# Sketched attention and a squared-ReLU MLP on one core: denominators from a Gram matrix, x made transposed in 32x32 array tiles, and one written order for all engines

## The chip, the core and the metric

The kernel runs on one core of a Trainium2 chip. The core has five engines with instruction queues of their own: PE (matrix multiply; it writes to PSUM), DVE and ACT (both read PSUM and SBUF), POOL (does not read PSUM here) and SP (issues DMAs). ACT and POOL issue DMAs too. Engines wait for one another by semaphores, and each runs its own instructions in order. The metric is the device time of one execution in microseconds; the number for a kernel is the median over runs.

## The reference, cut to what matters

```python
batch, n_heads, seq, head_dim, r = 4, 4, 1088, 32, 8      # q, k, v: float32

def phi(x):
    a = einsum('rd,bhsd->bhsr', S1, x)
    b = einsum('rd,bhsd->bhsr', S2, x)
    return einsum('bhsi,bhsj->bhsij', a, b).reshape(..., r * r)

q_p, k_p = phi(q), phi(k)
kv  = einsum('bhsf,bhsd->bhfd', k_p, v)
z   = sum(k_p, axis=2)
num = einsum('bhsf,bhfd->bhsd', q_p, kv)
den = einsum('bhsf,bhf->bhs', q_p, z)[..., None] + 1e-06
x   = (num / den) transposed to [4352, 128]                # 4 heads x 32
out = square(maximum(x @ w_in, 0)) @ w_out                 # d_ff 2048
```

Since `z` summed over the keys is the 8x8 matrix G of products of `a` and `b` of the keys, `den` is also a(q)ᵀ G b(q).

## The kernel before

Of 1088 = 34 x 32 tokens of a batch, 32 x 32 go in two chunks of 512 and the last 2 x 32 of every batch are collected in a ninth chunk of 256 (`ci` 0 to 8).

**Keys** (`k_stage`, once per batch). DVE transposes k in 32x32 blocks (L149, L154). PE projects it on S1 and S2 (L175, f32, outputs on 64 partitions). ACT copies the `a` half out of PSUM (L190) and DVE multiplies it with the `b` half into 64 features (L191). v is copied beside a column of ones (`v_pad`, L198 and L200, POOL after batch 0), and PE sums features times [v, 1] over the keys with the features stationary (L209, 128 rows by 32 columns of the array, 33 moving columns): the 33rd column is z. POOL (ACT and DVE in batch 0) spreads the sums into `KV` (L229).

**Queries** (`q_feat`). DVE transposes q (L149, L154), PE projects with the stationary Wq and 512 moving columns (L260), DVE transposes the result out of PSUM (L266), forms the 64 features (L268) and transposes them (L276) into `qp`.

**Output of attention** (`q_out`). PE multiplies qp and KV in 64x64 tiles (L298, 66 moving columns: two heads of 32 values and a denominator). DVE adds 1e-6, takes reciprocals and scales (L312 to L315) into bf16, PE transposes (L324), ACT copies to `xT` (L330).

**MLP** (`f_stage`, nine chunks, eight units of two 128-wide blocks of d_ff). PE makes h (L355, bf16, 512 moving columns), ACT applies Relu from PSUM to bf16 (L362), DVE squares four blocks at a time (L366, 2048 columns), PE accumulates the output (L371, 16 matmuls per square), ACT copies it out (L381), and four DMAs on SP store it (L384; the last chunk's are L389). `h_ps` has two buffers of two PSUM banks, `r_sb` and `g_sb` three each, `o_ps` one.

**Order.** A generator runs attention steps between MLP units (80 steps spread over the units); the framework's scheduler orders each engine, with chains for the matmuls of a step. Loads go on SP batch by batch: k, six pieces of v, q. POOL issues the weights (L111, L112), which are converted to bf16 on the way, after a one-element copy from v of batch 0 (L110); another from the weights into k of batch 1 (L113) holds the later loads on SP until the weights are in.

Of the kernel before, what the change touches and what calls it, by code (L numbers as in the profile page):

```python
# [19 lines left out]

@with_exitstack
def kernel(
# [11 lines left out]
    nc = tc.nc  # L34
    NOSYNC = mybir.DependencyInfo(mybir.DependencyClass.NoSync, mybir.DependencyReason.DATA)

    def chain(insts):

        for x, y in zip(insts, insts[1:]):
            tc.add_manual_dep(y.ins, x.ins.name, NOSYNC, reason="chain")  # L40

# [3 lines left out]
    F = r * r  # L45
# [4 lines left out]
    VW = D + 1  # L50
    assert (B, H, D, r, NJ) == (4, 4, 32, 8, 34)

    consts = ctx.enter_context(tc.tile_pool(name="consts", bufs=1))
    kin = ctx.enter_context(tc.tile_pool(name="kin", bufs=1))
    kTp = ctx.enter_context(tc.tile_pool(name="kTp", bufs=2))
    vin = ctx.enter_context(tc.tile_pool(name="vin", bufs=1))
    kab_pool = ctx.enter_context(tc.tile_pool(name="kab", bufs=2))
    kp_pool = ctx.enter_context(tc.tile_pool(name="kp", bufs=2))
    a_pool = ctx.enter_context(tc.tile_pool(name="arep", bufs=3))
    qp_pool = ctx.enter_context(tc.tile_pool(name="qp", bufs=3))  # L60
    den_pool = ctx.enter_context(tc.tile_pool(name="den", bufs=3))
    xb_pool = ctx.enter_context(tc.tile_pool(name="xb", bufs=2))
    xT_pool = ctx.enter_context(tc.tile_pool(name="xT", bufs=4))
    r_pool = ctx.enter_context(tc.tile_pool(name="r", bufs=3))
    g_pool = ctx.enter_context(tc.tile_pool(name="g", bufs=3))
    osb_pool = ctx.enter_context(tc.tile_pool(name="osb", bufs=2))
    ps_h = ctx.enter_context(tc.tile_pool(name="ps_h", bufs=2, space=PSUM))
    ps_o = ctx.enter_context(tc.tile_pool(name="ps_o", bufs=1, space=PSUM))
    ps_m = ctx.enter_context(tc.tile_pool(name="ps_m", bufs=3, space=PSUM))

    warm = consts.tile([128, 1], F32)
    nc.vector.memset(warm, 0.0)
    nc.scalar.activation(warm, warm, ACTF.Relu)
# [5 lines left out]
    nc.scalar.dma_start(out=S12[:r, 0, :], in_=S1)  # L79
    nc.scalar.dma_start(out=S12[r:, 0, :], in_=S2)  # L80

    kin_t, qin_t, vraw, vpad = {}, {}, {}, {}
    for b in range(B):
        kin_t[b] = kin.tile([128, NJ, D], F32, tag=f"k{b}", name="k_in")
        qin_t[b] = kin.tile([128, NJ, D], F32, tag=f"q{b}", name="q_in")
        vraw[b] = vin.tile([128, H, NLO + 1, D], F32, tag=f"v{b}", name="v_in")
        vpad[b] = vin.tile([128, H, NLO + 1, VW], F32, tag=f"vp{b}", name="v_pad")
    w_in_sb = consts.tile([128, C_TILES, 128], BF16)
    w_out_sb = consts.tile([128, C_TILES, 128], BF16)

    def load(b):
        nc.sync.dma_start(out=kin_t[b], in_=k[b].rearrange("h (t j) d -> (h t) j d", j=NJ))
        for h in range(H):
            vr = v[b, h].rearrange("(t j) d -> t j d", j=NJ)[:, : 4 * NLO, :]
            nc.sync.dma_start(  # L95
                out=vraw[b][:, h, :NLO, :],
                in_=vr.rearrange("t (i l) d -> i t (l d)", i=4),
            )
        for j2 in range(2):
            nc.sync.dma_start(  # L100
                out=vraw[b][32 * j2 : 32 * (j2 + 1), :, NLO, :],
                in_=v[b].rearrange("h (t j) d -> j t h d", j=NJ)[32 + j2],
            )
        nc.sync.dma_start(out=qin_t[b], in_=q[b].rearrange("h (t j) d -> (h t) j d", j=NJ))

    load(0)

    for b in range(B):
        nc.gpsimd.memset(vpad[b][:, :, :, D:VW], 1.0)
    nc.gpsimd.tensor_copy(w_in_sb[:1, 0, :1], vraw[0][:1, H - 1, 0, :1])  # L110
    nc.gpsimd.dma_start(out=w_in_sb, in_=moe_w_in.rearrange("d (ct c) -> d ct c", c=128))  # L111
    nc.gpsimd.dma_start(out=w_out_sb, in_=moe_w_out.rearrange("(ct c) d -> c ct d", c=128))  # L112
    nc.gpsimd.tensor_copy(kin_t[1][:1, 0, :1], w_in_sb[:1, 0, :1])  # L113
    for b in range(1, B):
        load(b)


    ident_b = consts.tile([128, 128], BF16)
    nc.vector.tensor_copy(ident_b, ident)
    mask = consts.tile([128, H], F32)  # L120
    nc.vector.memset(mask, 0.0)
    for h in range(H):
        nc.vector.memset(mask[32 * h : 32 * (h + 1), h : h + 1], 1.0)
    nc.vector.tensor_copy(
        S12[:, 1:, :], S12[:, 0:1, :].to_broadcast([2 * r, H - 1, D])
# [6 lines left out]
    nc.vector.tensor_tensor(  # L132
        out=Wk,
        in0=T_ps[:, None, : 2 * r].to_broadcast([128, H, 2 * r]),
        in1=mask[:, :, None].to_broadcast([128, H, 2 * r]),
        op=ALU.mult,
    )
    Wq = consts.tile([128, H, 32], F32)
    nc.vector.memset(Wq, 0.0)
    nc.vector.tensor_copy(Wq[:, :, : 2 * r], Wk)  # L140
    KV = consts.tile([128, B, 2, 2, VW], F32)
    nc.vector.memset(KV, 0.0)
    KV0 = 360
    qT_rem = consts.tile([128, B, 64], F32)
    qT_all = {}

    def block_transpose(dst, dst_rem, src):
        pin(
            nc.vector.transpose(  # L149
                dst.rearrange("p (l h t) -> p l h t", l=NLO, h=4),  # L150
# [3 lines left out]
        pin(nc.vector.transpose(dst_rem, src[:, 4 * NLO :, :]))  # L154


    def k_stage(b):

        kt = kTp.tile([128, S], F32, tag="kT", name="kT")
        block_transpose(  # L160
            kt[:, :1024], kt[:, 1024:].rearrange("p (j t) -> p j t", j=2), kin_t.pop(b)
        )
        vt = vpad[b]
        eng = nc.scalar.copy if b == 0 else nc.gpsimd.tensor_copy
        yield
        tiles = ([(m, 128) for m in range(4)], [(m, 128) for m in range(4)] + [(4, 64)])
        kks, kps, seqs = {}, {}, ([], [])

        def project(gi):
            kks[gi] = kk = ps_m.tile([128, 512], F32, tag="m", name="kab_ps")  # L170
            for m, P in tiles[gi]:
                c0 = (4 * gi + m) * 128
                for c in range(P // 64):
                    seqs[gi].append(
                        nc.tensor.matmul(  # L175
                            kk[64 * c : 64 * c + 64, m * 64 : (m + 1) * 64],
                            kt[:, c0 + 64 * c : c0 + 64 * c + 64],
                            Wk.rearrange("p h x -> p (h x)"),
                            start=True,
                            stop=True,  # L180
                        )
                    )

        def features(gi):
            kk = kks[gi]
            ka = kab_pool.tile([128, 5 * H, r], F32, tag="ka", name="ka")
            kps[gi] = kp = kp_pool.tile([128, 5 * H, r, r], F32, tag="kp", name="kp")
            for P, g0, g1 in ((128, 0, 4 * H), (64, 4 * H, 5 * H))[: gi + 1]:
                kabv = kk[:P, g0 * 2 * r : g1 * 2 * r].rearrange("p (g x) -> p g x", x=2 * r)
                nc.scalar.copy(ka[:P, g0:g1], kabv[:, :, :r])  # L190
                nc.vector.tensor_tensor(  # L191
                    out=kp[:P, g0:g1],
                    in0=ka[:P, g0:g1, :, None].to_broadcast([P, g1 - g0, r, r]),
                    in1=kabv[:, :, None, r:].to_broadcast([P, g1 - g0, r, r]),
                    op=ALU.mult,
                )
            n0 = 4 * gi
            pin(eng(vt[:, :, n0 : n0 + 4, :D], vraw[b][:, :, n0 : n0 + 4, :]))  # L198
            if gi:
                pin(eng(vt[:64, :, NLO, :D], vraw[b][:64, :, NLO, :]))  # L200

        def sums(gi):
            kp, seq = kps[gi], seqs[gi]
            kv = kks[0][:, KV0 : KV0 + 2 * VW].rearrange("p (f w) -> p f w", f=2)
            for m, P in tiles[gi]:
                for f in range(2):
                    for h in range(H):
                        seq.append(
                            nc.tensor.matmul(  # L209
                                kv[32 * h : 32 * h + 32, f],  # L210
                                kp[:P, m * H + h, 4 * f : 4 * f + 4].rearrange(
                                    "p i j -> p (i j)"
                                ),
                                vt[:P, h, 4 * gi + m, :],
                                start=(gi == 0 and m == 0 and f == 0),
                                stop=(gi == 1 and m == len(tiles[1]) - 1 and f == 1),
                            )
                        )
            if gi:
                if b:  # L220
# [243 lines left out]
```

## Time and profile before

| what | value |
| --- | --- |
| median of 3 runs | 145.01 us (144.13 to 145.67) |
| profiled execution | 145.95 us, of which the span is 143.8 us |
| granted TensorE clock | 0.997 |
| moved by DMA | 8.78 MB read, 2.23 MB written |

The span runs from the first instruction to the end of the last store; the execution's own time is 2.15 us longer. "Busy" is the union of an engine's instructions, so overlapped ones count once. In a group's row the two numbers before the second bar are the busy time of the group and the mean of one instruction in ns, and after it stands the idle time just before the group and what ended it. An f32 matmul appears as two records.

| group | count | mean ns of one |
| --- | --- | --- |
| h, L355, 512 columns bf16 | 112 records | 390 |
| output, L371, 128 columns bf16 | 544 | 219 |
| nd, L298, 64x64 tiles, 66 columns f32 | 544 | 234 |
| key sums, L209, 128x32 tiles, 33 columns f32 | 512 | 210 |
| Relu, L362, 1024 columns | 64 | 1031 |
| square, L366, 2048 columns | 32 | 1221 |
| key features, L191, 1024 columns f32 | 8 | 1210 |
| query features, L268, 1024 columns f32 | 8 | 1296 |
| query feature transposes, L276, 1024 columns f32 | 8 | 1238 |

Matmuls overlap, so their rate is read from rows of the timeline, in which consecutive instructions of a kind are merged, and not from these means.

### The profile page before, as it was taken

Reading aid. Unit: us, or ns where it says so; the run is one execution under the profiler, and the core shown is the slowest. Engines: PE = TensorE matmul, PEld = TensorE weight load, DVE = VectorE, ACT = ScalarE, POOL = GpSimd, SP = SyncE. Lnnn points to the kernel's source line nnn. Section 1 sums busy time; section 2 is a strip of 40 time slices with the busy share of each in tenths; the row PEclk is TensorE's granted clock in tenths of the full one; section 3 lists DMA queues with packets and bytes.
Section 4 is the critical chain, followed back from the end, with each engine's and each line's share of the span. In section 5 each row is a group of like instructions: output and inputs, shape, how many; then the busy total and the mean of one; then the engine's idle time right before and its main releaser. Section 6 shows DMA issues by size and latency. Waiting matters only on the chain.

```text
span 143.8 us, 4505 instructions
## 1 busy us (share of the span) xinstructions
PE 106.3 (74%) x1981; PEld 71.8 (50%) x1997; DVE 101.1 (70%) x159; ACT 81.0 (56%) x112; POOL 17.0 (12%) x35
## 2 busy tenths in 40 slices
PE   0243946795896988799889698996969967989840
PEld 0233434154573746476456275763817643656720
DVE  2534753679899399886995997799579575655530
ACT  4002201282839286756973929557394558999840
POOL 2005000510009400002900000050000000000000
PEclk9999999999999999999999999999999999999998
DMA  4463995248446300200020002000110020011021
GB/s 152 96 193 107 226 316 125 52 175 263 147 111 185 102 1 5 59 21 5 0 58 20 0 5 73 5 5 0 39 39 0 23 55 0 0 44 34 15 58 39
DMA packets 8531, 10.24 MB, mean 71 GB/s; under 512 B 4033, under 2 KB 6337, under 8 KB 8513
## 3 DMA queue, kind: packets, MB, share of 16 engines
q1 hardware_dynamic: 6112, 8.85, 21.2%
q0 software_dynamic: 2208, 1.05, 5.5%
q8 instruction: 15, 0.25, 0.7%
q10 hardware_dynamic: 192, 0.07, 0.2%
q14 instruction: 4, 0.02, 0.0%
HBM read 8.78 MB, written 2.23 MB: 77 GB/s over the span
## 4 chain that ended last, share of the span: by engine, by line
DVE 26%; PE 23%; DMA 16%; issue 14%; ACT 11%; POOL 4%; SPq 2%; another core or an unknown queue 1%; ACTq 0%; POOLq 0%
DMA v_in<-in_v_dram 16%; DVE g_sb L366 11%; PE o_ps L371 10%; ACT r_sb L362 9%; PE h_ps L355 4%; DVE qf L268 4%; DVE qp L276 4%; DVE ab L266 3%; POOL KV L229 3%; PE nd_ps L298 3%; SPq L95 2%; DVE kT L149 2%; PE pr_ps L260 2%; PE kab_ps L209 2%; PE kab_ps L175 1%
## 5 line engine op out<-in xcount | busy, mean ns | idle before, releaser
L362 ACT ACTIVATE r_sb<-h_ps 128x1024 bf16<-128x1024 f32 (+1 forms) x72 | 66.6, 983 | 23.2 <-remote 8.9
L366 DVE TENSOR_TENSOR g_sb<-r_sb 128x2048 bf16<-128x2048 bf16 (+1 forms) x36 | 41.6, 1162 | 13.7 <-ACT r_sb L362 13.6
L355 PE MATMUL h_ps<-xT,w_in_sb 128*128 128x512 bf16 (+1 forms) x128 | 38.5, 376 | 9.8 <-ACT r_sb L362 8.1
L371 PE MATMUL o_ps<-w_out_sb,g_sb 128*128 128x128 bf16 x544 | 36.3, 219 | 4.5 <-DVE g_sb L366 3.8
L371 PEld LDWEIGHTS <-g_sb 128*128 128x128 bf16 x544 | 31.5, 98 | 12.2 <-DVE g_sb L366 10.4
L355 PEld LDWEIGHTS <-w_in_sb 128*128 128x128 bf16 x144 | 12.7, 99 | 22.6 <-issue 18.5
L298 PE MATMUL nd_ps<-KV,qp 64*64 64x66 f32 x544 | 12.5, 234 | 3.4 <-DVE KV L229 2.1
L298 PEld LDWEIGHTS nd_ps<-KV,qp 64*64 64x64 f32 x544 | 10.6, 143 | 7.7 <-DVE KV L229 2.3
L229 POOL COPY KV<-kvs 32x66 f32<-32x66 f32 x12 | 6.6, 552 | 55.8 <-ACT kvs L222 55.3
L191 DVE TENSOR_TENSOR kp<-ka,kab_ps 128x1024 f32<-128x1024 f32 (+1 forms) x12 | 11.2, 941 | 2.4 <-ACT ka L190 2.4
L381 ACT COPY osb<-o_ps 128x512 f32<-128x512 f32 (+1 forms) x9 | 5.1, 565 | 11.8 <-PE o_ps L371 11.8
L266 DVE STREAM_TRANSPOSE ab<-pr_ps 128x512 f32<-128x512 f32 (+1 forms) x9 | 6.2, 684 | 7.9 <-PE pr_ps L260 7.9
L260 PE MATMUL pr_ps<-qT,Wq 128*128 128x512 f32 x16 | 10.4, 738 | 1.2 <-DVE qT_rem L154 1.1
L268 DVE TENSOR_TENSOR qf<-ab 128x1024 f32<-128x1024 f32 (+1 forms) x9 | 11.1, 1228 | 0.2
L209 PE MATMUL kab_ps<-v_pad,kp 128*32 128x33 f32 (+1 forms) x576 | 8.4, 210 | 3.5 <-ACT v_pad L198 3.1
L276 DVE STREAM_TRANSPOSE qp<-qf 128x1024 f32<-128x1024 f32 (+1 forms) x9 | 10.6, 1180 | 0.1
L209 PEld LDWEIGHTS kab_ps<-v_pad,kp 128*32 128x32 f32 (+1 forms) x576 | 7.1, 121 | 7.2 <-ACT v_pad L198 4.8
L330 ACT COPY xT<-xT_ps 128x512 bf16<-128x512 bf16 (+1 forms) x9 | 5.1, 562 | 4.7 <-PE xT_ps L324 4.5
L190 ACT COPY ka<-kab_ps 128x128 f32<-128x128 f32 (+1 forms) x12 | 2.8, 234 | 8.5 <-PE kab_ps L175 5.1
L149 DVE STREAM_TRANSPOSE qT<-q_in 128x1024 f32<-128x1024 f32 x4 | 4.9, 1234 | 3.5 <-DMA q_in<-in_q_dram 3.5
L175 PE MATMUL kab_ps<-Wk,kT 128*64 128x64 f32 x136 | 6.8, 250 | 0.7 <-DVE kT L154 0.4
L175 PEld LDWEIGHTS kab_ps<-Wk,kT 128*64 128x64 f32 x136 | 5.7, 159 | 2.8 <-PE h_ps L355 0.9
(42 smaller groups left out, 45.4 us busy)
## 6 DMA issues: line engine op xcount, KB each, us to landing
k_in<-in_k_dram SPq DMA_DIRECT2D x4, 544.0 KB, 7.3
q_in<-in_q_dram SPq DMA_DIRECT2D x4, 544.0 KB, 7.0
v_in<-in_v_dram SPq DMA_DIRECT2D x16, 128.0 KB
out_dram<-osb SPq DMA_DIRECT2D x32, 64.0 KB, 1.7
w_out_sb<-in_moe_w_out_dram POOLq DMA_DIRECT2D x1, 512.0 KB, 13.0
w_in_sb<-in_moe_w_in_dram POOLq DMA_DIRECT2D x1, 512.0 KB, 14.2
v_in<-in_v_dram SPq DMA_DIRECT2D x8, 16.0 KB, 7.9
out_dram<-osb SPq DMA_DIRECT2D x2, 32.0 KB
```

What stands on the lines that cost most here:

```text
L175: nc.tensor.matmul(kk[64 * c : 64 * c + 64, m * 64 : (m + 1) * 64], kt[:, c0 + 64 * c : c0 + 64 * c + 64], Wk.rearrange("p h x -> p (h x)" ...
L191: nc.vector.tensor_tensor(out=kp[:P, g0:g1], in0=ka[:P, g0:g1, :, None].to_broadcast([P, g1 - g0, r, r]), in1=kabv[:, :, None, r:].to_broa ...
L209: nc.tensor.matmul(kv[32 * h : 32 * h + 32, f], kp[:P, m * H + h, 4 * f : 4 * f + 4].rearrange("p i j -> p (i j)"), vt[:P, h, 4 * gi + m, ...
L229: eng(KV[rows, b, :, h % 2, :], src[rows])
L260: nc.tensor.matmul(pr[:, :N], Wq.rearrange("p h x -> p (h x)"), cols, start=True, stop=True)
L268: nc.vector.tensor_tensor(out=qf[:, :nj], in0=ab[:, :nj, :r, None].to_broadcast([128, nj, r, r]), in1=ab[:, :nj, None, r : 2 * r].to_broad ...
L276: nc.vector.transpose(qp[:, :, :N].rearrange("p f (j t) -> p j f t", t=32), qf[:, :nj].rearrange("p j (f i) k -> p j f (i k)", f=2),)
L298: nc.tensor.matmul(nds[g][64 * c : 64 * c + 64, m * 2 * VW : (m + 1) * 2 * VW], qp[rows, f, c0 : c0 + 64], KV[rows, bs[2 * m + c], f].rear ...
L355: nc.tensor.matmul(h_ps[:, u, :N], w_in_sb[:, 4 * g4 + 2 * g2 + u, :], xT[:, :N], start=True, stop=True,)
L362: nc.scalar.activation(rt[:, 2 * g2 : 2 * g2 + 2, :N], h_ps[:, :, :N], ACTF.Relu)
L366: nc.vector.tensor_mul(gt[:, :, :N], rt[:, :, :N], rt[:, :, :N])
L371: nc.tensor.matmul(o_ps[:, m, :], gt[:, u, m * 128 : (m + 1) * 128], w_out_sb[:, ct, :], start=(ct == 0 and m == 0), stop=(ct == C_TILES - ...
```

## The change

Every engine's computing instructions are now pinned in the order of one written list, `ORDER`, with the engine of copies, squares, Relus and some multiplies chosen item by item (`@A` ACT, `@V` DVE, `@G` POOL). The items are `name.batch-or-chunk.part`.

- **Keys:** both halves are copied out of PSUM (`kc`, ACT) before the features are formed (`kp`). The sums (`kv`) have v stationary and 64 feature columns moving, so they come out as [32 values, 64 features] per head; a further matmul per tile adds up the 32x32 Gram matrix of b and a for all heads, of which only the four diagonal 8x8 blocks are used. There is no v_pad and no column of ones. `kt` copies the sums out four times side by side, `kr` multiplies by the identity (f32) to put features on partitions in four copies, `kx` copies that to `KV`. S2 as a block-diagonal matrix times the Gram matrix gives, masked, a third set of projection columns (`wc`), specific to the batch.
- **Queries:** the projection (`qa`) has q stationary (64 tokens) and 96 moving columns: a, G b (through `wc`) and b for four heads, so tokens come out on partitions and no transpose out of PSUM is needed. `qc` copies it out. `dt` multiplies a by the second set, `dr` adds up with 1e-6 and takes the reciprocal, `da` scales a by it. Features (`qf`) and their transposes (`qp`) follow, for both chunks of a batch together.
- **Attention output:** `nd` has KV stationary in 32x32 tiles and 256 token columns moving, eight tiles in turn (two row groups, four column groups). x comes out transposed and normalized; `xe` copies it to bf16.
- **MLP:** as before, but squares go two blocks at a time (1024 columns). r and g have six buffers. DVE has 11 of the 72 Relus and three of the nine copies out, ACT 17 of the 72 squares. The last chunk's store is eight DMAs instead of four.
- **Loads:** k and q of all batches are issued on SP at once, after S1. v goes on POOL's queue, before the weights for batch 0 and after them for the others. The one-element copies are gone.

```diff
+ORDER = """
+kT.0 ka.0.0 kc.0.0@A ka.0.1 kc.0.1@A kp.0.0 kp.0.1 kv.0.0 kv.0.1 qT.0 kt.0@A kr.0 kx.0@A kT.1
+wc.0 qa.0.0 qc.0.0@A qa.0.1 qT.1 qc.0.1@A ka.1.0 ka.1.1 kc.1.0@A dt.0.0@V dr.0.0 da.0.0@V
+dt.0.1@V qf.0.0 dr.0.1 da.0.1@V kc.1.1@A qf.0.1 qp.0.0 qp.0.1 nd.0.0 kp.1.0 kv.1.0 xe.0.0@A
+M.0.0 R.0.0@A M.0.1 kp.1.1 qT.2 kv.1.1 kt.1@A R.0.1@V S.0.0@V M.0.2 R.0.2@A kr.1 wc.1 S.0.1@V
...
-    load(0)
-    nc.gpsimd.tensor_copy(w_in_sb[:1, 0, :1], vraw[0][:1, H - 1, 0, :1])
-    nc.gpsimd.tensor_copy(kin_t[1][:1, 0, :1], w_in_sb[:1, 0, :1])
...
+    for b in range(B):
+        nc.sync.dma_start(out=kin_t[b], in_=k[b].rearrange("h (t j) d -> (h t) j d", j=NJ))
+        nc.sync.dma_start(out=qin_t[b], in_=q[b].rearrange("h (t j) d -> (h t) j d", j=NJ))
+    load_v(0)
+    w_in_sb = consts.tile([128, C_TILES, 128], BF16)
+    nc.gpsimd.dma_start(out=w_in_sb, in_=moe_w_in.rearrange("d (ct c) -> d ct c", c=128))
+    w_out_sb = consts.tile([128, C_TILES, 128], BF16)
+    nc.gpsimd.dma_start(out=w_out_sb, in_=moe_w_out.rearrange("(ct c) d -> c ct d", c=128))
+    for b in range(1, B):
+        load_v(b)
...
+    def kv(b, gi, eng):
...
+        for m in range(4 + gi):
+            first, last = gi == 0 and m == 0, gi == 1 and m == 4
+            for h in range(H):
+                pin(
+                    nc.tensor.matmul(
+                        acc[32 * h : 32 * h + 32, :64],
+                        vraw[b][:P, h, 4 * gi + m, :],
+                        t[:P, m * H + h].rearrange("p i j -> p (i j)"),
...
+            a, b2 = (s[:P, x, m * H : m * H + H].rearrange("p h i -> p (h i)") for x in range(2))
+            pin(
+                nc.tensor.matmul(
+                    acc[:32, 64:96],
+                    b2,
+                    a,
...
+    def kr(b, eng):
...
+        pin(
+            nc.tensor.matmul(
+                T["acc", b][:, 96:128],
+                S2bd.rearrange("p h d -> p (h d)"),
+                Gs[:, b],
...
+    def wc(b, eng):
+        pin(
+            nc.vector.tensor_tensor(
+                out=Wq[:, b, :, r : 2 * r],
+                in0=T["acc", b][:, 96:128].rearrange("p (h x) -> p h x", h=H),
+                in1=mask[:, :, None].to_broadcast([128, H, r]),
...
+                    nc.tensor.matmul(
+                        t[64 * c : 64 * c + 64, m * H * W : (m + 1) * H * W],
+                        cols,
+                        Wq[:, be].rearrange("p h x -> p (h x)"),
...
-                                nds[g][64 * c : 64 * c + 64, m * 2 * VW : (m + 1) * 2 * VW],
-                                qp[rows, f, c0 : c0 + 64],
-                                KV[rows, bs[2 * m + c], f].rearrange("p x w -> p (x w)"),
...
+        for c0, c1, be in cols:
+            for f in range(2):
+                for h in range(H):
+                    for l in range(2):
+                        rows = slice(64 * c + 32 * l, 64 * c + 32 * l + 32)
+                        pin(
+                            nc.tensor.matmul(
+                                nds[l][32 * h : 32 * h + 32, c0:c1],
+                                KV[rows, be, f, 32 * h : 32 * h + 32],
+                                src[rows, 2 * h + f, c0:c1],
+                                start=(f == 0),
+                                stop=(f == 1),
...
+        if eng == "A":
+            pin(nc.scalar.activation(t[:, :, :N], h[:, :, :N], ACTF.Relu))
+        else:
+            pin(nc.vector.tensor_scalar_max(t[:, :, :N], h[:, :, :N], 0.0))
...
+        if eng == "A":
+            pin(nc.scalar.activation(t[:, :, :N], s, ACTF.Square))
+        else:
+            pin(nc.vector.tensor_mul(t[:, :, :N], s, s))
...
+    for item in ORDER.split():
+        name, _, eng = item.partition("@")
+        op, *args = name.split(".")
+        OPS[op](*map(int, args), eng)
```

## The prediction

> **What bounds the kernel now.** I began with the page's busy shares and slices.
>
> ```profile
> span 143.8 us, 4505 instructions
> PE 106.3 (74%) x1981; PEld 71.8 (50%) x1997; DVE 101.1 (70%) x159; ACT 81.0 (56%) x112; POOL 17.0 (12%) x35
> PE   0243946795896988799889698996969967989840
> DVE  2534753679899399886995997799579575655530
> ACT  4002201282839286756973929557394558999840
> ```
>
> No engine is full over the span. The first seven slices are thin and the rest dense, so I split the time at the first MoE matmul (26.9 us) and at the last (139.4 us) and asked for each engine's busy time (first line the start, second the main stretch, third the tail).
>
> ```profile
> 0.00:26.90 26.90, 12.06 (x252) 8.04 (x253) 12.35 (x31) 4.43 (x11) 3.06 (x14) 1.00 0.69 164
> 26.90:139.40 112.50, 94.29 (x1730) 63.73 (x1746) 88.71 (x129) 76.16 (x100) 13.90 (x22) 1.00 0.18 51
> 139.40:143.80 4.40, 0.00 (x0) 0.00 (x0) 0.00 (x0) 0.37 (x1) 0.00 (x0) 0.89 0.13 32
> ```
>
> The columns after the length are PE, PEld, DVE, ACT and POOL, then clock, DMA share and GB/s. Over 112.5 us PE is at 84%, DVE at 79%, ACT at 68%: three engines take turns waiting. The waits say for what.
>
> ```profile
> DVE g_sb L366 <- ACT r_sb L362: 13.6, 18, 1.2
> ACT osb L381 <- PE o_ps L371: 11.8, 7, 3.6
> PE h_ps L355 <- ACT r_sb L362: 8.1, 19, 0.8
> ACT r_sb L362 <- PE nd_ps L298: 7.6, 3, 2.9
> ```
>
> The main stretch is therefore a loop h, r, g, o, with bursts of attention work pushed into it. The start is another matter; its timeline ends with the weights.
>
> ```profile
> 26.81 0.17 POOL L113 CAST k_in<-w_in_sb 1x1 f32<-1x1 bf16 x1 [13.65 <-DMA w_in_sb<-in_moe_w_in_dram]
> 26.89 0.59 PE L355 MATMUL h_ps<-xT,w_in_sb 128*128 128x512 bf16 x1 [0.67 <-DMA w_in_sb<-in_moe_w_in_dram]
> ```
>
> The one-element copy at L110 held the weights until v's first batch had landed (11.2 us), and they took 14.2 us more.
>
> **Unit prices**, from the groups kept apart by shape (mean ns last before the bar's end) and from single rows of the timeline:
>
> ```profile
> L362 ACT ACTIVATE r_sb<-h_ps 128x1024 bf16<-128x1024 f32 x64 | 62.3, 1031 | 22.8 <-remote 8.9 <-PE nd_ps L298 7.6 <-PE h_ps L355 4.4
> L366 DVE TENSOR_TENSOR g_sb<-r_sb 128x1024 bf16<-128x1024 bf16 x4 | 2.8, 690 | 2.3 <-ACT r_sb L362 2.3
> L266 DVE STREAM_TRANSPOSE ab<-pr_ps 128x512 f32<-128x512 f32 x8 | 5.7, 714 | 6.9 <-PE pr_ps L260 6.9
> ```
>
> **The start, step by step.** S1 now goes ahead of k on SP: one issue of such a load took 0.61 us on ACT's queue, so k lands at 4.5 + 0.6 = 5.1. The new memsets on DVE (about 2.5 us, the largest row being 0.50 for 528 columns) fit before that. kT 1.4 gives 6.5; ka at 2.2 for 34 records (row at 6.57) feeds kc from 7.7; kp takes 1.2 + 1.2 + 0.4, to 10.9; kv's end to 11.6, if v has landed by 11.1 as now. Then kt 0.6, kr 0.5 and kx 0.4 give 13.1. wc stands on DVE behind qT (1.5) and kT of batch 1 (1.4), so 14.0: that wait is covered only if k of batch 1 has landed. qa (about 1.6 at the early, slower matmul rate, where pr took 2.04 against 1.02 later) and qc 0.5 give 16.1. DVE then has dt, dr and da twice (0.95 each by the small rows), two qf (1.23) and two qp (1.24): 6.9, to 23.0. On PE the first MoE matmul is pinned behind nd and behind kv of batch 1, which needs kp (1.2, to 24.2) and v of batch 1: 26.0. From the DMA side: k and q (4.46 MB), v of two batches (1.1 MB) and the weights (1.05 MB as written) are 6.6 MB; v of batch 1 is now last in POOL's queue, behind both weights. At 259 GB/s, the rate of 15 to 20 us, that is 25.5 us, landing near 27.5. I take 28, so 1.1 us later than now, but with both chunks of batch 0 through qp and batch 1 half through.
>
> The Trainium skill has a price for POOL's transfers: "DMA: Bandwidth & Descriptors", section "Anatomy of one DMA — SWDGE (gpsimd) path", fits 2.0 us plus bytes/436e3 per us. By it 0.5 MB of weights lands in 3.2 us, where the row here says 14.2; with the page's price v of batch 1 would be in by about 10 us and the sum 2 us shorter (26.0 instead of 28). I go by the row.
>
> **PE in the main stretch.** By lines the stretch holds nd 9.97, ka 4.63, kv 5.75, pr 6.99 and xT 3.03, together 30.4 us.
> - xT goes: -3.03.
> - nd: 64 records of 66 columns took 1.17 us, 18 ns each. pr, which has the array to itself, took 1.02 us for two records of 512 columns, 1.0 ns a column, so 66 columns would be 66 ns: four 64x64 tiles overlapped 3.6-fold. The new nd has 32 records of 256 columns a chunk on eight 32x32 tiles: 256/3.6 = 71 ns each at today's overlap (2.3 us), 32 ns if all eight overlap (1.0 us). I take 41 ns, 1.3 us, because consecutive records change tile as they do now. Seven chunks and chunk 8's 64 short records (1.2): 10.3.
> - qa: 104 records at the ka price (1.23/34 = 36 ns) times 96/64: 5.6 for pr's 6.99.
> - ka has one batch less here: 3.1. kv: half the records at 64 instead of 33 columns (13.3 ns becomes 26) plus 54 Gram records: 6.0. kr: 1.8, new.
>
> Sum 26.8, so PE falls from 94.3 to 90.7.
>
> **ACT.** It keeps 57 of 64 full Relus (1.03) and 4 small ones (0.60): 61.1. It takes 17 squares; no row shows one here, so bounds are the bf16-to-bf16 DVE row (0.69) and the Relu row (1.03), and I take 1.03, the same engine and size: 16.2. osb 3.3, xe 3.1, kc 2.5, kt 1.7, kx 0.4, qc 1.9 by the copy rows (0.38 for 256 columns, 0.59 for 512). Sum 90.2; such sums exceed the union of busy time by 3.5% now (79 against 76.2), so 87, up 11.
>
> **DVE.** 50 full squares at 0.62 (half of 1.15 back to back is 0.58, alone 0.69) and 5 small: 32.8. Eleven Relus and three osb out of PSUM: L266 costs 1.03 ns a column between its two sizes, so 1.24 for 1024 and 0.71 for 512: 13.7. kT and qT 5.7, kp 7.0, qf 7.9, qp 7.9 (each less what the start now did). dt, dr, da, qc, xe, kx, wc: 10.7, in place of ab 5.9 and den, rec, xb 9.9. Sum 85.7, about 84 as a union, down 5. POOL loses v_pad and KV (13.9 us busy); beside v_pad copies a g_sb took 1.50 instead of 1.23 and a qf 1.67, which also goes. Six small POOL multiplies are off the path, unless POOL is still issuing v then.
>
> So PE 91, ACT 87, DVE 84: near equal. The length is the largest over its busy share. The whole stretch has 84% now; the best 10 us have 93% (PE 60 to 70, DVE 90 to 100). I take 92%: squares come in halves, r and g have six buffers instead of three, and two engines empty h. 90.7/0.92 = 98.6.
>
> **Tail.** The last chunk leaves in four DMAs on each of two queues instead of two; an issue took 0.43 to 0.64 us, so 4.4 becomes 5.5.
>
> Sum: 28 + 98.6 + 5.5 = 132.1 span. The profiled run took 145.95 for 143.8 of span (+2.15) and is 0.94 over the median of 145.01: 133.3, rounded to **133**.
>
> **Rivals.**
> 1. *Starved start (slower).* All loads are issued at once, and PE's first MoE matmul waits for v of batch 1, the last in its queue. If the stream runs at the mean of the first four slices (152, 96, 193, 107: 137 GB/s), 6.6 MB take 48 us, the first MoE matmul comes near 50, and the run takes 133 + 22 = 155. It turns slower once that matmul comes after 41 us, a rate below 170. For it: those slices. Against: in them few loads were outstanding (SP issued them one by one), and with more the rate was 205 to 343. 0.11.
> 2. *The waits stay.* Fixed orders stall one another, PE stays at 81%: 112 us, total 146, no change. For it: each engine's loads are now so even that any stall hits all. 0.10.
> 3. *Tiles overlap no more than today.* nd at 2.3 us, eight more us on PE: 141, still faster. Eight tiles need four moving streams per row group; kv's 128x32 tiles show four at 12 ns for 33 columns, so it is unlikely to be worse. 0.12.
>
> My own case has 0.67. A measurement of this kernel tells about 1% from no change; faster by more gets the first case, most of 3 and little of 2: 0.81; within 1%: 0.06; slower: 0.13. The range goes down to 126 (95% busy, nd at 32 ns: 89/0.95 = 94, 27 + 94 + 5) and up to 146, case 2.
>
> **What would show it.** First MoE matmul at 26 to 30 us (41 or later: rival 1). 32 nd records in 1.0 to 1.5 us (2.3: rival 3). In the main stretch PE near 91, ACT 87, DVE 84, each over 85% of it. A busy sum 5 us off in any engine, or a stretch beyond 106 us with these sums right, makes the working wrong.

## The result, and the profile after

The changed kernel takes 129.23 us (median of four runs, 127.96 to 129.92) beside 145.34 for the kernel before on the same chip: a ratio of 0.887, 95% interval 0.876 to 0.898. The forecast was 133 in a range of 126 to 146. The profiled execution took 128.9 us with a span of 127.1, so 1.8 us lie around the span. Some executions, three of e12's six among them, ran longer at a lower granted clock; ratios are of the others.

The busy shares and slices of the changed kernel, with the granted clock:

```profile
span 127.1 us, 4039 instructions
...
PE 100.2 (79%) x1729; PEld 72.7 (57%) x1729; DVE 101.9 (80%) x187; ACT 87.1 (69%) x130; POOL 22.6 (18%) x38
...
PE   0062187307999998999998999999899999799920
...
DVE  6359304999569999999999998999999799879800
ACT  4220003400449998989999997999799999599910
...
PEclk9999999965579999999999999999999999999997
DMA  2999999965610000210030020002002003020121
```

From the eleventh slice on PE's row, and from the thirteenth on the rows of DVE and ACT too, are nearly all nines and eights, up to the last slices, where before they alternated. The ten slices ahead of that are thin, DMA is full in most of them, and the clock (PEclk) falls to half while PE stands idle and is still there when PE comes back. The same three stretches as before, cut at the first MoE matmul (32.76) and at the last one's end:

```profile
0.00:32.76 32.76, 13.29 (x269) 10.77 (x270) 20.87 (x52) 6.26 (x19) 16.84 (x30) 0.90 0.93 224
32.76:121.50 88.74, 86.87 (x1462) 61.97 (x1460) 80.98 (x136) 80.48 (x110) 5.75 (x9) 0.98 0.12 30
121.50:127.10 5.60, 0.00 (x0) 0.00 (x0) 0.00 (x0) 0.37 (x1) 0.00 (x0) 0.84 0.13 35
```

| us | before | forecast | measured |
| --- | --- | --- | --- |
| start, to the first MoE matmul | 26.9 | 28 | 32.8 |
| main stretch | 112.5 | 98.6 | 88.7 |
| of it PE, DVE, ACT busy | 94.3, 88.7, 76.2 | 90.7, 84, 87 | 86.9, 81.0, 80.5 |
| PE's share | 84% | 92% | 98% |
| tail | 4.4 | 5.5 | 5.6 |

The start is 6 us longer than before and the main stretch 24 us shorter. The waits that carried the reading of before are nearly gone; those that answer to them in the list of waits are

```profile
PE acc_ps L280 <- DMA v_in<-in_v_dram: 5.4, 3, 2.2
...
ACT r_sb L506 <- PE h_ps L492: 4.7, 8, 1.7
...
PEld L527 <- DVE g_sb L517: 0.9, 3, 0.5
...
PE h_ps L492 <- ACT r_sb L506: 0.7, 1, 0.7
...
DVE g_sb L517 <- ACT r_sb L506: 0.3, 1, 0.3
```

The 13.6 us that DVE's squares waited for ACT's Relus have shrunk to 0.3, the 8.1 us that PE waited for these Relus to 0.7, and what is left of PE's waiting is in the start, where the key sums (L280) wait for v. Rows of the timeline of the start show the chain (start and length in us, then the idle time and what ended it):

```profile
11.47 0.42 PE L280 MATMUL acc_ps<-kp,v_in 128*32 128x64 f32 x2 [1.33 <-DMA v_in<-in_v_dram]
...
14.12 0.42 PE L280 MATMUL acc_ps<-kp,v_in 128*32 128x64 f32 x2 [2.23 <-DMA v_in<-in_v_dram]
...
16.43 0.31 PE L280 MATMUL acc_ps<-kp,v_in 128*32 128x64 f32 x1 [1.89 <-DMA v_in<-in_v_dram]
...
20.66 0.19 DVE L338 TENSOR_TENSOR Wq<-acc_ps,mask 128x32 f32<-128x32 f32 x1 [6.96 <-PE acc_ps L324]
...
20.91 1.54 PE L380 MATMUL qab_ps<-Wq,qT 128*64 128x96 f32 x32 [0.28 <-DVE Wq L338]
...
29.45 1.96 PE L469 MATMUL nd_ps<-qp,KV 32*32 32x256 f32 x32 [5.96 <-DVE qp L445]
...
32.76 1.89 PE L492 MATMUL h_ps<-xT,w_in_sb 128*128 128x512 bf16 x4
...
38.07 1.09 PE L469 MATMUL nd_ps<-qp,KV 32*32 32x256 f32 x32
```

The four pieces of v, one per head, come one by one, the last at 16.4 us; until then the keys' features, done at 11.1, lie there, and DVE stands idle for 7 us before wc (L338). The key sums that could only start with the last piece take another 2.9 us (16.4 to 19.3). The rows at 29.45 and 32.76 ran at half clock: the same 32 nd records take 1.96 us there and 1.09 in the last row.

### The profile page after: what moved, and what is told of

The parts are those of the page before. It is cut to its first block, busy times and chain, and to the rows that moved or that the text cites. A ratio compares the mean times of both kernels' runs of the same rounds, so it can differ in the third digit from the quotient of the medians.

```text
span 127.1 us, 4039 instructions
## 1 busy us (share of the span) xinstructions
PE 100.2 (79%) x1729; PEld 72.7 (57%) x1729; DVE 101.9 (80%) x187; ACT 87.1 (69%) x130; POOL 22.6 (18%) x38
## 4 chain that ended last, share of the span: by engine, by line
PE 39%; DVE 30%; DMA 10%; issue 8%; ACT 6%; POOL 2%; POOLq 0%; ACTq 0%; DVEq 0%
PE h_ps L492 14%; PE o_ps L527 13%; DMA v_in<-in_v_dram 10%; DVE g_sb L517 9%; PE acc_ps L280 5%; DVE qf L432 5%; PE nd_ps L469 4%; ACT r_sb L506 4%; DVE qp L445 4%; DVE kp L262 2%; DVE kT L212 2%; POOL v_in L131 2%; PE kr_ps L315 1%; DVE rec L412 1%; DVE den L407 1%
## 5 line engine op out<-in xcount | busy, mean ns | idle before, releaser
L492 PE MATMUL h_ps<-xT,w_in_sb 128*128 128x512 bf16 (+1 forms) x144 | 38.8, 375 | 0.8 <-ACT r_sb L506 0.7
L527 PE MATMUL o_ps<-w_out_sb,g_sb 128*128 128x128 bf16 x544 | 36.6, 219 | 0.4 <-DVE g_sb L517 0.4
L517 DVE TENSOR_TENSOR g_sb<-r_sb 128x1024 bf16<-128x1024 bf16 (+1 forms) x55 | 35.0, 668 | 0.5 <-ACT r_sb L506 0.3
L492 PEld LDWEIGHTS <-w_in_sb 128*128 128x128 bf16 x144 | 12.1, 100 | 9.7 <-issue 4.5
L515 ACT ACTIVATE g_sb<-r_sb 128x1024 bf16<-128x1024 bf16 (+1 forms) x17 | 16.8, 985 | 0.2
L469 PE MATMUL nd_ps<-qp,KV 32*32 32x256 f32 (+1 forms) x384 | 11.1, 340 | 6.7 <-DVE qp L445 6.7
L280 PE MATMUL acc_ps<-kp,v_in 128*32 128x64 f32 x288 | 10.5, 270 | 6.2 <-DMA v_in<-in_v_dram 5.4
L131 POOL DMA_DIRECT2D v_in<-in_v_dram x16 | 11.2, 706 | 15.3 <-DMA v_in<-in_v_dram 7.5
L508 DVE TENSOR_SCALAR r_sb<-h_ps 128x1024 bf16<-128x1024 f32 (+1 forms) x11 | 11.3, 1027 | 3.0 <-PE h_ps L492 3.0
L280 PEld LDWEIGHTS acc_ps<-kp,v_in 128*32 128x32 f32 x288 | 8.2, 127 | 9.2 <-DMA v_in<-in_v_dram 6.2
L262 DVE TENSOR_TENSOR kp<-kab 128x1024 f32<-128x1024 f32 (+1 forms) x12 | 10.7, 943 | 1.5 <-ACT kab L251 1.5
L432 DVE TENSOR_TENSOR qf<-aq,qab 128x1024 f32<-128x1024 f32 (+1 forms) x9 | 10.3, 1142 | 0.1
L290 PE MATMUL acc_ps<-kab 128*32 128x32 f32 x72 | 8.9, 223 | 0.0
## 6 DMA issues: line engine op xcount, KB each, us to landing
w_in_sb<-in_moe_w_in_dram POOLq DMA_DIRECT2D x1, 512.0 KB, 15.1
w_out_sb<-in_moe_w_out_dram POOLq DMA_DIRECT2D x1, 512.0 KB, 20.1
```

The costliest lines, as they stand in the source:

```text
L131: nc.gpsimd.dma_start(out=vraw[b][:, h, :NLO, :], in_=vr.rearrange("t (i l) d -> i t (l d)", i=4),)
L262: nc.vector.tensor_tensor(out=t[:P, g0:g1], in0=s[:P, 0, g0:g1, :, None].to_broadcast([P, g1 - g0, r, r]), in1=s[:P, 1, g0:g1, None, :].to ...
L280: nc.tensor.matmul(acc[32 * h : 32 * h + 32, :64], vraw[b][:P, h, 4 * gi + m, :], t[:P, m * H + h].rearrange("p i j -> p (i j)"), start=first,
L290: nc.tensor.matmul(acc[:32, 64:96], b2, a, start=False, stop=last,)
L432: nc.vector.tensor_tensor(out=t[:, :n], in0=T["aq", b, i][:, :n, :, None].to_broadcast([128, n, r, r]), in1=s[:, :n, None, 2 * r :].to_bro ...
L469: nc.tensor.matmul(nds[l][32 * h : 32 * h + 32, c0:c1], KV[rows, be, f, 32 * h : 32 * h + 32], src[rows, 2 * h + f, c0:c1], start=(f == 0) ...
```

## Experiments

Theories: (A) the written order keeps PE fed; (B) the new split of Relus and squares between ACT and DVE does it; (C) the new attention steps do it. For the start: (D) v of batch 0 is late, (E) the DMA engines are full and something is always late. All times are beside runs of the kernel before in the same job (145.3 to 146.1 us).

### e1: no pins

```diff
-    pin = tc.keep_in_program_order
+    def pin(inst):
+        return inst
```

> The changed kernel with its list as program order, but without the pins: the framework's scheduler orders each engine. Theory A (the written order keeps PE fed, 86.9 us of busy PE in a main stretch of 88.7): PE falls back towards the 84% of before, 87/0.86 = 101 us for the stretch, total 135 to 142. Theory B (the new split of Relus and squares between ACT and DVE does it) and theory C (the new attention steps do it): 128 to 131, as the changed kernel.

135.74 us (135.36 to 136.44), ratio 0.931, interval 0.926 to 0.936. Its main stretch, by the view of stretches:

```profile
35.80:128.03 92.23, 88.94 (x1463) 62.16 (x1460) 77.66 (x129) 80.44 (x111) 3.44 (x6) 0.99 0.10 25
```

The pins are worth 6.5 us: 3.5 in the main stretch and 3.0 in the start (the first MoE matmul comes at 35.8). In the start wc comes as early as with the pins (20.7), but then DVE does two key features (kp) of batch 1 ahead of the last transposes of batch 0, and nd starts at 32.5 instead of 29.4; some 0.7 us of it is the projection of the queries, which ran slower (2.83 us for 1.54). But PE stays at 96%, not at 86%: the number fits A's range, its working does not. Even as program order alone the list leaves most of the gain in the main stretch (92.2 us, from 112.5).

### e2: another pinned order

```diff
-        ... items of ORDER from M.0.0 on
+        ... M(n), R(n), S(n-1), O(n-2); attention items spread evenly between the units
```

> The changed kernel from its first MoE matmul on in another pinned order: units in the plain sequence M(n), R(n), S(n-1), O(n-2), attention items in their own order spread evenly between units, engines of all items as in the changed kernel. Start the same. Theory A: 134 to 142, with PE's idle time of 2 us growing to 8 or more. Theories B and C: 128 to 131.

177.61 us (176.34 to 178.86), ratio 1.216: slower than the kernel before. Every theory expected less. Two of its largest waits, those of ACT and DVE, are

```profile
ACT r_sb L510 <- PE h_ps L496: 44.4, 29, 7.0
...
DVE g_sb L521 <- ACT r_sb L510: 38.2, 29, 3.5
```

and its main stretch is

```profile
38.30:170.66 132.36, 96.65 (x1379) 63.31 (x1372) 81.15 (x131) 82.03 (x109) 3.04 (x6) 0.92 0.07 17
```

Two things differ from the expectation. The attention items are not spread evenly: 14 stand in one block right ahead of M.3.0 and 21 ahead of M.5.0, and none within the rest of chunks 3 and 5 (from M.0.1 on, the list of the changed kernel has at most 11 in one place). And the start is not the same: nine more items stand ahead of the first MoE matmul, which comes at 38.3. So e2 is the price of this order, not of every plain one.

A fixed order gains nothing by being fixed. Where its items do not fit, each engine waits for the one ahead, and no scheduler moves work into the hole.

### e3 and e5: the split of before, with pins and without

```diff
-... R.0.1@V S.0.0@V ... S.0.2@A ... E.4@V ...
+... R.0.1@A S.0.0@V ... S.0.2@V ... E.4@A ...
```

> The changed kernel with all Relus and output copies on ACT and all squares on DVE, as in the kernel before; places in the order kept. Sums for the main stretch: ACT 80.5 - 16.8 + 9.6 + 1.8 = 75, DVE 81.0 - 13.4 + 10 = 78, both under PE's 87. Theory A with PE as the bound: 128 to 132. Theory B: 134 or more, with PE waiting for h buffers.

> As e1 (no pins), with e3's split (all Relus and output copies on ACT, all squares on DVE). e3 lost 11 us, but its places were written for the other split. If the split itself is worth that, the scheduler cannot mend it: 142 to 147, some 7 or more over e1's 135.7. If e3 lost because places and split no longer fitted each other, the scheduler's order fits either: 134 to 138, as e1.

With the pins (e3) 140.46 us (140.02 to 141.33), ratio 0.963; without them (e5) 135.92 (135.08 to 136.85), ratio 0.935, interval 0.929 to 0.942, the same as e1. The waits of e3 and the main stretch of e5:

```profile
DVE g_sb L521 <- ACT r_sb L510: 17.0, 15, 3.8
...
ACT r_sb L510 <- PE h_ps L496: 14.6, 17, 3.5
```

```profile
36.10:128.62 92.52, 86.86 (x1444) 62.01 (x1460) 74.04 (x132) 76.08 (x107) 4.68 (x6) 0.99 0.10 25
```

B falls. The old split has less work in sum (DVE 74, ACT 76) and, left to the scheduler, does as well as the new one. e3 alone would have been taken for 11 us of the split. Since the split costs nothing in e5, I put the 11 us down to places that were written for other engines; a pinned order written for the old split was not tried.

### e4: half of the output product

```diff
-        for i in range(2):
+        for i in range(1):
             ct = 2 * u + i
```

> The changed kernel without every second block of d_ff in the output product (half of the w_out matmuls left out; Relus, squares and everything else stay): PE loses 272 of 544 matmuls, about 16 us. If PE alone is the bound, 113. If PE is the bound with DVE and ACT (81 us each) close behind: the stretch falls to about 81/0.95 = 85, total 125. If the fixed order's waits are the bound: 128 to 130.

126.13 and 128.6 us, beside 127.96 to 129.92 for the changed kernel. Two executions are too few to settle it by the total, so the answer is taken from the main stretch of the profiled one:

```profile
32.80:118.58 85.78, 75.62 (x1190) 46.59 (x1188) 80.77 (x136) 79.63 (x110) 6.22 (x9) 0.99 0.13 32
```

PE loses 11 us of busy time and the stretch 3: DVE is now at 94% of it and ACT at 93%. That fits the stretch of the second expectation (85): PE is the bound, with the two others some 3 us behind. The total lies between the second and the third, and one profile does not exclude that waits of the fixed order, which e4 leaves as they are, hold part of the stretch.

### e12: the steps without the list

```diff
-        ... ORDER from M.0.0 on, pinned
+        ... unit after unit M, R, S, O, attention items spread evenly; no pins; split as before
```

> The changed kernel's steps, buffers and loads without its order: the list up to the first MoE matmul, then unit after unit M, R, S, O with the attention items spread evenly between them in the manner of the kernel before, no pins, all Relus and output copies on ACT and all squares on DVE. The framework's scheduler orders the engines, as in the kernel before. The main stretch was 112.5 us before, 88.7 changed, 92.2 and 92.5 in e1 and e5, which have no pins but the list as program order. Theory H (the list, pinned or not, is what closes PE's idle time): 104 to 113 in the stretch, total 145 to 154. Theory I (the new steps and the halves do it): 91 to 95, total 133 to 138. Between: both.

Three executions took 152.74 to 153.86 us, a ratio of 1.060, interval 1.049 to 1.070. The profiled one is among the other three, at 161.85; its main stretch was

```profile
35.80:154.50 118.70, 110.57 (x1462) 67.52 (x1460) 77.66 (x132) 77.80 (x107) 2.82 (x6) 0.90 0.08 20
```

with the clock at half from 80 to 90 us and for parts of 115 to 125. Its start (35.8) and tail (5.6) lie outside these parts; with them the span of 151.5 us of a shorter execution leaves an estimated 110 us for the main stretch: theory H. e5 and e12 differ only in the sequence of the items: the same items on the same engines, both ordered by the scheduler, take 92.5 us from the list and about 110 from this plain program. So the new steps, halves and six buffers are not enough by themselves, and C falls as the cause by itself.

Here too the items are not spread evenly: as in e2, 14 stand in one block ahead of M.3.0 and 21 ahead of M.5.0. Whether a plain program without such blocks, or the old steps under a list as good, would have done as well as the list was not tried.

### e8: tiles in pairs

```diff
-            for f in range(2):
-                for h in range(H):
-                    for l in range(2):
+            for h in range(H):
+                for l in range(2):
+                    for f in range(2):
```

> The changed kernel with the two accumulating matmuls of a 32x32 tile next to each other, instead of eight tiles in turn and then again. If the overlap (32 nd records in 1.09 us, 34 ns each, where one alone would be about 255) needs neighbours in different tiles, nd goes to about 2 us, eight more us of PE: 134 to 138. If PE reaches past the neighbour, no change: 128 to 130.

128.77 us (127.84 and 129.71), no change. 32 nd records take 1.14 us instead of 1.09:

```profile
36.74 1.14 PE L469 MATMUL nd_ps<-qp,KV 32*32 32x256 f32 x32
```

So the overlap does not come from the turn of tiles, which was my reason for taking 41 ns a record. At 34 ns against an estimated 255 for one alone (1.0 ns a column, from the old projection) it is 7.5-fold on eight tiles.

### e6 and e7: v on SP's queue

```diff
         nc.sync.dma_start(out=kin_t[b], ...)
+        if b == 0:
+            load_v(0, nc.sync)
         nc.sync.dma_start(out=qin_t[b], ...)
```

> The changed kernel with v of batch 0 on SP's queue between k and q of batch 0, instead of first on POOL's. Theory D (the start is held by that v: its fourth piece landed at 16.4 us, and the key sums waited for it): the first MoE matmul moves from 32.8 to 27 to 28.5, total 124 to 126. Theory E (the DMA engines are full until 28 us, so whatever goes ahead pushes something else back that the start needs, the weights or v of batch 1): it stays at 31 to 33, total 128 to 130.

> As e6, and v of batch 1 on SP too, behind q of batch 1, so POOL's queue begins with the weights. Theory D: 124 to 126 as e6, or 0.5 better if v of batch 1 is the next thing late. Theory E: 127 to 130.

Worse: 134.40 us (133.95 to 134.89) and 133.38 (133.01 to 134.24), with the first MoE matmul at 38.8 and 38.7 us. Neither theory expected a loss. SP's issues in e6:

```profile
1.60 4.23 SPq L131 DMA_DIRECT2D v_in<-in_v_dram  x4
5.88 4.13 SPq L136 DMA_DIRECT2D v_in<-in_v_dram  x2
10.05 0.43 SPq L145 DMA_DIRECT2D q_in<-in_q_dram  x1
12.44 0.35 SPq L142 DMA_DIRECT2D k_in<-in_k_dram  x1
```

In the changed kernel q of batch 0 is issued at 1.60 and k of batch 1 at 2.45. Here they come at 10.05 and 12.44. The six issues of v ahead of q took 8.4 us, 3.3 of it waiting until k and pieces of v had landed, and k of batch 1 waited another 2.0 for v (SP's waits name k_in ahead of L131 and v_in ahead of L136 and L142). That such an issue waits because it shares a completion semaphore with an earlier DMA is my reading; the profile shows the wait and not the semaphore. DVE then waits 12.2 us for q of batch 0, whose transpose starts at 22.6, and 1.2 for q of batch 1, at 27.1: these two loads took more than 12 us from issue to landing, where one of the changed kernel's took 5.6. Moving the late transfer made the next two late.

### e9, e10, e11: hold the later loads, keep PE busy

```diff
+    for t in (kin_t[2], qin_t[2], kin_t[3], qin_t[3]):
+        nc.gpsimd.tensor_copy(t[:1, 0, :1], vraw[0][:1, H - 1, 0, :1])
...
+        for i in range(14):                     # e10, e11: ahead of the first nd
+            pin(nc.tensor.matmul(t[:, i % 2, :], w_in_sb[:, 0, :], ...))
```

> The changed kernel with k and q of batches 2 and 3 held on SP until the fourth piece of v of batch 0 has landed (four one-element copies on POOL behind the weights' issue). Theory F (the DMA engines are full, the queues take turns, and v of batch 0 shares them with four k and four q loads, 4.5 MB): with half of them held, v is in after 2.2 + 0.6 MB at 290 GB/s, near 12 us instead of 16.4, the first MoE matmul comes at 28 to 29.5 and the total is 124.5 to 126.5. Rival: the weights, q of batch 2 or v of batch 1 become late in its place: 128 to 130.

> The changed kernel with 14 extra bf16 matmuls of 512 columns on PE (their result is read by nobody) between the projections of batch 1 and the first nd, where PE stood idle from 23.5 to 29.4 us and the granted clock was 0.50 from 28 to 36. Theory G: the idle time costs the clock; with work in it nd of chunk 0 takes 1.1 us instead of 1.96 and four MoE matmuls 1.04 instead of 1.89, total 125.5 to 127.5. Rival: DVE and ACT hide it, 128.5 to 129.5, or the extra matmuls are late themselves and cost up to 2 us.

> e9 and e10 together. If both theories hold and add up: 121.5 to 124. If only one does, as that one.

| | total us | ratio, interval | first MoE matmul |
| --- | --- | --- | --- |
| changed | 129.23 | 0.887, 0.876 to 0.898 | 32.8 |
| e9 | 127.43 | 0.877, 0.873 to 0.881 | 32.1 |
| e10 | 127.62 | 0.878, 0.875 to 0.881 | 31.9 |
| e11 | 127.80 | 0.881, 0.877 to 0.886 | 31.3 |

Each median is 1.4 to 1.8 us lower, but the intervals overlap with that of the changed kernel, so a gain is not shown for any of them alone; they do not add up either. In e9 the last of the four pieces of v is there at 14.1 us instead of 16.4, as theory F has it in direction but only half in size, and matmuls that follow ran slower than in the changed kernel:

```profile
19.50 2.83 PE L387 MATMUL qab_ps<-Wq,qT 128*64 128x96 f32 x32 [0.28 <-DVE Wq L345]
```

The same 32 records took 1.54 us at 20.91 in the changed kernel. wc came 1.4 us earlier than there, the first nd and the first MoE matmul 0.6: most of the 2.3 us went back to PE's own pace. Why PE was slower there no run shows; the granted clock is 1.00 in both profiles. In e11 the chain of waits names the rival: v of batch 1, whose issue stood behind the hold, landed at 30.1 ("DMA v_in" from 17.07 for 12.98 us), and PE's key sums ahead of the first MoE matmul waited 0.6 us for it.

For e10 the stretches of 2 us (PE first after the length, clock third from the end), the changed kernel and then e10:

```profile
26.00:28.00 2.00, 0.00 (x0) 0.00 (x0) 2.00 (x2) 0.00 (x0) 0.95 (x2) 0.58 0.53 107
...
30.00:32.00 2.00, 2.00 (x57) 1.01 (x43) 2.00 (x4) 0.52 (x2) 2.00 (x4) 0.50 0.55 156
...
34.00:36.00 2.00, 2.00 (x50) 1.42 (x49) 1.31 (x2) 0.86 (x1) 0.11 (x1) 0.50 0.51 155
```

```profile
28.00:30.00 2.00, 0.91 (x32) 0.57 (x32) 2.00 (x3) 0.00 (x0) 2.00 (x4) 0.93 0.50 83
30.00:32.00 2.00, 2.00 (x56) 1.48 (x42) 2.00 (x4) 0.65 (x2) 2.00 (x4) 0.50 0.61 165
...
34.00:36.00 2.00, 1.85 (x39) 1.30 (x31) 1.51 (x4) 1.36 (x4) 0.28 (x1) 1.00 0.57 152
```

In stretches of 0.1 us the clock of the changed kernel falls at 26.3 and is back at 36.6; with the extra matmuls it falls at 29.7 and is back at 33.2, and nd of chunk 0 takes 1.44 instead of 1.96. They ended at 26.3, 2.8 us ahead of nd, and the clock fell again after that gap, 0.6 us after nd had begun.

## Why the prediction was right, and where it was not

- **Direction, size, cause of the bound.** Right: all three engines come out within 6.4 us of one another, PE ahead, and e4 points to that order with some 3 us between the first and the second. That the point was only 4 us too long is in part luck: the main stretch was forecast 9.9 us too long and the start 4.8 too short.
- **Main stretch, 98.6 us: the busy share of 92% was mis-sized.** It is 98%, worth 5.7 of the 9.9 us (86.9/0.92 = 94.4). The reasons given for it, halves, six buffers, two engines that empty h, do not do it by themselves: e12 has the first two and about 110 us, e5 lacks the third and has 92.5. What does it is the list's sequence of items, mostly even as a mere program order (e1, e5), the last 3.5 us by the pins together with the engines chosen for them. Whether the list needs the halves and the six buffers was not tried.
- **PE's sum, 90.7 us.** 86.9 measured, the other 4.2 us of the stretch. nd with 9.2 (for 10.3), qa with 5.0 (for 5.6), ka with 2.6 (for 3.1) and kv with 5.4 (for 6.0) were priced high; kr with its masked product 2.9 (for 1.8) low. That is 1.7 of the 3.8 us; the rest is matmuls of different groups that overlap and are counted once (the groups sum to 13.6 us more than PE's busy time, 10.9 before).
- **ACT 87 and DVE 84** are 80.5 and 81.0. ACT's is 6.5 off, so by the prediction's own sign (a busy sum 5 us off in any engine) this part of the working was wrong. Most prices hold (a full square on ACT 1062 ns for 1030, a Relu on DVE 1222 for 1240; a full square on DVE was 693 for 620). What failed is the step from the sum to the busy time: ACT's measured means again sum to about 90, but instructions that overlap count once, and that took 10% off in a full engine instead of 3.5%.
- **Start, 28 us: the step "if v has landed by 11.1 as now" failed.** v landed at 16.4. The working let the weights and v of batch 1 share the DMA engines with k and q, but not v of batch 0, which now shares them with four k and four q loads; with half of them held (e9) it lands 2.3 us earlier. wc, forecast for 14.0, came at 20.7: 5.3 us for v, and more because the key sums, counted as done 0.5 us after v, took 2.9. From wc to the first MoE matmul the chain took 12.1 us, as forecast (14.0 to 26.0). At 32.8 that matmul lies outside the 26 to 30 that the prediction named. The DMA side of the sum (6.6 MB near 27.5 at 259 GB/s) was close: the slices show 263 to 330 GB/s from 3 to 22 us.
- **The clock after an idle PE** was not in the sum at all: some 3 us of PE's time at half clock, from nd (0.87), the first four MoE matmuls (0.85) and the key sums of batch 1 (3.2 us, where those of batch 2 took 1.75). How much of it reaches the total is open: e10, which takes part of it away, has a median 1.6 us lower, within the intervals.
- **POOL's transfers.** The price of "DMA: Bandwidth & Descriptors", "Anatomy of one DMA — SWDGE (gpsimd) path", in the Trainium skill would, as an estimate, have had 0.5 MB of weights in within 3.2 us. Here w_in took 15.1 us and w_out 20.1 from issue to landing. The row of before (14.2) was the better guide, and it too was low for w_out.
- **Rivals.** The starved start came in part: the first MoE matmul at 32.8, far from the 41 at which it decides. The waits stayed in e2 and in e12 (33.4 us of DVE's squares for ACT's Relus in its longer, profiled execution), not in the change. Tiles overlap 7.5-fold.
- **Tail** 5.6 for 5.5.

## What to carry to other kernels

When three engines are evenly loaded, the order of the work can decide between 89 and 132 us of main stretch for nearly the same instructions (the changed kernel and e2), and an order belongs to the engines it was written for: test a split of work with the order free, not with the old places kept. In a start where the DMA engines are full, moving one late load forward can make others late (e6, e7); count what shares the engines and the queue with the transfer that the chain needs first.

## What the runs showed of the hardware that was not expected

- In the changed kernel PE had no matmul from 23.5 to 29.4 us. The granted clock fell to 0.50 at 26.3 and stayed there until 36.5, although PE was busy from 29.4 on without a break. "TensorE: Matmul & The Clock Gate", Part 1 of the Trainium skill, gives about 3.4 us of sustained work for the way back. From PE's return it took 7.1 us here, 4.0 in e10 and 7.7 in e11; why they differ no run shows. After a gap of 2.8 us (e10, e11) the clock fell as well.
- A granted clock of 1.00 in the profile does not mean that PE is at its later pace. In the changed kernel the same 34 records of ka took 2.18 us in the start and 1.21 later, both with 1.00:

```profile
6.86 2.18 PE L233 MATMUL kab_ps<-Wk,kT 128*64 128x64 f32 x34 [3.11 <-DVE kT L212]
...
22.28 1.21 PE L233 MATMUL kab_ps<-Wk,kT 128*64 128x64 f32 x34
```

- Two accumulating f32 matmuls on one 32x32 tile in a row cost no more than two on different tiles (1.14 and 1.09 us for 32 records).
